# Reordering the start of an attention kernel: K transposes ahead of x, half of V behind a swap, and w2 in pieces

## The chip, the cores and the metric

The kernel runs on one core of one Trainium2 chip. The metric is the time of one execution on the device in microseconds (us). The profile's span, from the first to the last instruction, is 1.8 us shorter than that time. PE is TensorE, PEld its weight loads, DVE VectorE, ACT ScalarE, POOL GpSimd; SPq is the queue of SyncE, which issues most DMAs.

## The reference

```
xn  = layernorm(A_x)                                   # 2048 x 640
q   = xn @ wq                                          # 32 heads of 192
p   = softmax(q @ k_cache.T / sqrt(192))               # 2048 keys per head
s   = (p @ v_cache, heads side by side) @ wo
g   = silu((silu(xn @ w1) * (xn @ w3)) @ w2)
out = A_x + s * g
```

All inputs are bfloat16. The part with w1, w3 and w2 uses the same normalised x as the attention.

## The kernel before

The kernel walks 32 heads x 4 query blocks of 512 rows x 8 pairs of key tiles. For each pair TensorE computes scores, ScalarE the exponential, and TensorE the product with V. At the start of each query block TensorE also computes the projection of the next head ("line 424"), from the normalised and transposed x (`xnT`) and from a copy with its two 64-row halves swapped (`xnS`).

Head 0 has to be started from nothing. Its order is written by hand (shortened here; cuts are marked with dots):

```python
def head_start():
    load_x(0, 0, 2); load_x(0, 2, 4)      # x block 0, SyncE's queue
    load_k0(0)                            # kn: first half of head 0's K
    load_w0()                             # GpSimd's queue
    load_k0(1)
    load_x(1)
    load_v(0)                             # both halves of head 0's V
    turn_over(40)                         # 40 matmuls that only warm TensorE up ("fillers")
    ...                                   # layer norm of x block 0 on DVE, ACT, POOL
    pk0 = ...
    ln_turn(0, 0, nc.scalar.copy)         # transpose x rows 0-255 on TensorE; ScalarE copies (line 354)
    turn_over(4)
    turn_k0(pk0, 0, (0, 1))               # transpose K (line 271)
    turn_over(4)
    ln_turn(0, 1, nc.vector.tensor_copy)  # x rows 256-511
    turn_k0(pk0, 0, (2, 3))
    turn_over(4)
    turn_k0(pk1, 1, (0, 1))
    swap_halves(0)                        # xnS <- xnT, two DMAs on SyncE's queue
    copy_k0(nc.scalar.copy, pk0, 0, 0); copy_k0(nc.scalar.copy, pk0, 0, 1)
    copy_k0(nc.vector.tensor_copy, pk1, 1, 0)
    for g in range(2, NQB):
        load_x(g)                         # x blocks 2 and 3
    project_first()                       # head 0, query block 0 (line 391)
    ...
    ln_norm(1, 0, nc.vector); ln_norm(1, 1, nc.vector)
    ln_turn_dma(1, 0); ln_turn_dma(1, 1)  # x block 1, first half: transposed by DMA into xnT
    ln_stats(1, 3)
```

Later, in query block 0 of head 0: `ln_stats(2, 0)` (VectorE, needs x block 2) stands in program order ahead of the cast of head 1's first projection (line 429); that cast frees a buffer in PSUM, the memory that TensorE writes its results to, that the next x transposes (line 354) want.

## Time and profile before

Three runs took 1942.91, 1943.74 and 1945.92 us. The kernel is limited by TensorE almost everywhere. First the share of TensorE and weight loads on the page of the kernel before, then busy time by stretch (columns: stretch, its length, then busy us and instruction count for PE, PEld, DVE, ACT, POOL; granted clock, DMA share, GB/s):

```profile
PE 1930.7 (99%) x27289; PEld 1318.9 (68%) x27289; DVE 654.6 (34%) x997; ACT 1181.4 (61%) x1278; POOL 282.0 (15%) x501
...
0.00:24.00 24.00, 19.02 (x223) 14.43 (x225) 15.76 (x49) 12.92 (x17) 8.64 (x16) 1.00 1.01 235
64.00:1624.00 1560.00, 1560.00 (x24100) 1064.46 (x24096) 533.77 (x742) 1104.27 (x1170) 254.88 (x455) 1.00 0.36 82
```

From 64 us to 1624 us TensorE has no gap at all, so no change to loads there can shorten anything. In the first 24 us it is idle for 5 us, while the DMA engines are saturated (share 1.01). The waits of PE in the first 30 us (who waits, for what: us, times, longest):

```profile
PE pk L568 <- POOL ident_bf masks.py:199: 2.8, 1, 2.8
PE ps L424 <- DMA xnS<-xnT: 1.1, 1, 1.1
PE pst L354 <- DVE xn L346: 0.7, 1, 0.7
```

The first line is the start-up before any filler can run. The second is the wait that the change aims at. Lines picked from the timeline around it (start, length, engine, line, operation; in brackets the idle time ahead of it and what ended it); here and below, lines in between are left out:

```profile
7.91 0.81 PE L354 MATMUL pst<-ident_bf,xn 128*128 128x128 bf16 x10 [0.69 <-DVE xn L346]
8.78 0.61 PE L271 MATMUL pk<-ident_bf,kn 128*128 128x128 bf16 x8
11.12 0.66 SPq L364 DMA_DIRECT2D xnS<-xnT  x1
11.82 0.62 SPq L365 DMA_DIRECT2D xnS<-xnT  x1
20.14 0.38 PE L424 MATMUL ps<-xnT,W 64*128 64x512 bf16 x1
21.58 0.39 PE L424 MATMUL ps<-xnS,W 64*128 64x512 bf16 x2 [1.07 <-DMA xnS<-xnT]
22.89 0.89 DVE L316 BATCH_NORM_STATS2 stats<-x_all 128x6 f32<-128x320 bf16 x2 [0.70 <-DMA x_all<-in_A_x_dram]
```

The swap is issued at 11.12 and 11.82 us and lands at 21.54 (9.7 us after its issue), behind V, whose second half lands at 18.10. TensorE arrives at head 1's projection at 20.14 and continues at 21.58.

### The profile page before, as it was taken

The page shows a single profiled execution, that of the slowest core. Times are in us where ns is not written, and L with a number is a line of the kernel's source. Part 1 is how long each engine was busy: PE and PEld are TensorE (multiplying, and loading weights), DVE is VectorE, ACT ScalarE, POOL GpSimd, SP SyncE. Part 2 cuts the span into 40 slices and gives each one's busy share as a digit, 9 for nine tenths or more (in the row PEclk, how much of TensorE's full clock was granted, in tenths as well). Part 3 has the DMA queues.
Part 4 walks back from the last instruction along what each step waited for, and adds up shares of the span by engine and source line. Part 5 has one row for each costly group of instructions (what it writes and reads, how often), then busy time and mean ns, then how long its engine had stood idle before and what let it go on. Part 6 is the DMA issues. An engine that isn't in the chain of part 4 may idle for free.

```text
span 1940.9 us, 59694 instructions
## 1 busy us (share of the span) xinstructions
PE 1930.7 (99%) x27289; PEld 1318.9 (68%) x27289; DVE 654.6 (34%) x997; ACT 1181.4 (61%) x1278; POOL 282.0 (15%) x501
## 2 busy tenths in 40 slices
PE   8999999999999999999999999999999999999998
PEld 6666666666666666666666666666666666577776
DVE  7333333333333333333333333333333334521111
ACT  5667776767776767776777777677767677210000
POOL 3111111111111111111111111111111110000000
PEclk9999999999999999999999999999999999999999
DMA  8743433323233424353434343434333220937883
GB/s 177 132 100 65 99 70 74 89 55 92 59 91 68 94 64 101 68 162 68 101 64 101 68 101 68 99 66 100 69 69 94 55 73 2 256 70 137 153 152 60
DMA packets 394563, 178.98 MB, mean 92 GB/s; under 512 B 341536, under 2 KB 382752, under 8 KB 394304
## 3 DMA queue, kind: packets, MB, share of 16 engines
q1 hardware_dynamic: 372384, 126.76, 30.6%
q0 software_dynamic: 19472, 45.71, 9.9%
q8 instruction: 215, 3.52, 0.8%
q10 hardware_dynamic: 2448, 2.62, 0.4%
q14 instruction: 44, 0.36, 0.1%
HBM read 52.82 MB, written 27.79 MB: 42 GB/s over the span
## 4 chain that ended last, share of the span: by engine, by line
PE 98%; DMA 1%; DVE 0%; ACT 0%; issue 0%; SPq 0%; DVEq 0%; ACTq 0%
PE obank L516 35%; PE st L487 33%; PE ps L424 14%; PE ps_s L111 11%; PE ps_f L728 3%; PE ps_gu L702 1%; PE st L488 1%; DMA xnS<-xnT 1%; PE ps L410 0%; DVE stats L316 0%; DMA x_all<-in_A_x_dram 0%; PE pst L354 0%; ACT pT L490 0%; ACT KW L277 0%; DVE osum L526 0%; PE pk L271 0%
## 5 line engine op out<-in xcount | busy, mean ns | idle before, releaser
L490 ACT ACTIVATE pT<-st 128x1024 bf16<-128x1024 f32 x1024 | 1047.2, 1023 | 250.8 <-PE st L488 234.8
L516 PEld LDWEIGHTS <-pT 64*128 64x128 bf16 x16384 | 713.8, 94 | 242.1 <-ACT pT L490 0.2
L516 PE MATMUL obank<-vt,pT 64*128 64x193 bf16 x16384 | 852.0, 243 | 0.0
L487 PE MATMUL st<-qC,KW 64*128 64x512 bf16 x2046 | 605.6, 376 | 0.0
L525 DVE COPY osum<-obank 128x772 f32<-128x772 f32 x128 | 123.1, 962 | 788.8 <-PE obank L516 788.8
L488 PE MATMUL st<-qB,KW 64*128 64x512 bf16 x1024 | 385.0, 376 | 0.0
L487 PE MATMUL st<-qA,KW 64*128 64x512 bf16 x1022 | 384.3, 376 | 0.4 <-ACT pT L490 0.3
L488 PE MATMUL st<-qC,KW 64*128 64x512 bf16 x1022 | 384.3, 376 | 0.0
L488 PE MATMUL st<-qA,KW 64*128 64x512 bf16 x1022 | 384.3, 376 | 0.0
L487 PEld LDWEIGHTS <-KW 64*128 64x128 bf16 x3068 | 278.0, 94 | 153.5 <-issue 2.1
L424 PE MATMUL ps<-xnT,W 64*128 64x512 bf16 x1280 | 297.2, 376 | 0.0
L424 PE MATMUL ps<-xnS,W 64*128 64x512 bf16 x1280 | 296.0, 376 | 1.1 <-DMA xnS<-xnT 1.1
L488 PEld LDWEIGHTS <-KW 64*128 64x128 bf16 x3068 | 278.0, 94 | 1.0 <-issue 0.6
L377 POOL DMA_DIRECT2D qC<-qA x124 | 65.4, 527 | 1286.9 <-DVE rl_all L532 1270.5
L430 ACT CAST qB<-ps 128x512 bf16<-128x512 f32 x131 | 76.8, 586 | 229.7 <-PE ps L424 224.2
L111 PE MATMUL ps_s<-wo_sb,oT 128*128 128x256 bf16 (+3 forms) x1536 | 208.8, 299 | 0.0
L424 PEld LDWEIGHTS <-W 64*128 64x128 bf16 x2560 | 122.9, 94 | 122.6 <-issue 1.4
L111 PEld LDWEIGHTS <-oT 128*128 128x128 bf16 x1536 | 148.4, 98 | 60.4
L526 DVE TENSOR_TENSOR osum<-osum,obank 128x772 f32<-128x772 f32 x128 | 122.7, 959 | 13.4
L533 DVE TENSOR_TENSOR ostage<-osum,rl_all 128x768 bf16<-128x768 f32 x128 | 122.7, 958 | 4.4
L465 DVE SCALAR_TENSOR_TENSOR hT<-pt,qB 64x512 bf16<-64x512 bf16 x64 | 43.8, 684 | 199.4 <-ACT pt L464 199.4
L429 DVE CAST qA<-ps 128x512 bf16<-128x512 f32 x131 | 90.6, 692 | 25.0 <-PE ps L410 7.2
(84 smaller groups left out, 623.6 us busy)
## 6 DMA issues: line engine op xcount, KB each, us to landing
vt<-in_A_v_cache_dram SPq DMA_DIRECT2D x64, 384.0 KB, 5.5
o_scr<-ostage SPq DMA_DIRECT2D x16, 1536.0 KB, 10.3
qC<-qA POOLq DMA_DIRECT2D x248, 64.0 KB, 2.0
qC<-qB POOLq DMA_DIRECT2D x124, 64.0 KB, 2.2
wo_sb<-in_A_wo_dram POOLq DMA_DIRECT2D x1, 7680.0 KB, 34.6
W<-in_A_wq_dram POOLq DMA_DIRECT2D x32, 160.0 KB, 3.4
W<-in_B_w_dram POOLq DMA_DIRECT2D x32, 80.0 KB, 3.2
W<-in_A_wq_dram POOLq DMA_DIRECT2D x32, 80.0 KB, 2.9
```

Of the source, the lines that this page charges most:

```text
L111: nc.tensor.matmul(ps[:, 0:w], lhsT=oT[:, k, :], rhs=wo_sb[:, k, c0:c1], start=(k == 0), stop=(k == OC - 1))
L377: nc.gpsimd.dma_start(out=qC[0:64, half, :], in_=qAB[half][64:P, :])
L424: nc.tensor.matmul(ps[:, r * 512:(r + 1) * 512], lhsT=W[rows, j, :], rhs=xs[rows, j // 2, qs], start=(j == 0), stop=(j == 2 * DC - 1))
L429: a = nc.vector.tensor_copy(out=qAB[0][:], in_=ps[:, 0:512])
L430: b = nc.scalar.copy(out=qAB[1][:], in_=ps[:, 512:1024])
L487: nc.tensor.matmul(st2[:, 0:512], lhsT=ka, rhs=qa, start=r == 0 and nr == 3, stop=r == nr - 1)
L488: nc.tensor.matmul(st2[:, 512:1024], lhsT=kb, rhs=qb2, start=r == 0 and nr == 3, stop=r == nr - 1)
L490: nc.scalar.activation(out=pT2[:], in_=st2[:], func=ACT.Exp, scale=att_scale)
L516: nc.tensor.matmul(obanks[r][:, j * 256:j * 256 + DH + 1], lhsT=pT2[r * 64:(r + 1) * 64, t * 512 + j * P:t * 512 + (j + 1) * P], rhs=vt[r ...
L525: nc.vector.tensor_copy(out=osum[:], in_=ov[0])
L526: nc.vector.tensor_tensor(out=osum[:], in0=osum[:], in1=ov[1], op=ALU.add)
L533: nc.vector.tensor_tensor(out=ostage[:, qb * 4:qb * 4 + 4, hg * DH:(hg + 1) * DH], in0=osum[:, :, 0:DH], in1=rl.unsqueeze(2).to_broadcast( ...
```

## The change

Three things: the K transposes of head 0's first half go ahead of the x transposes, with six fillers fewer, to use TensorE's idle gap; the second half of V is issued behind the swap; w2 (needed only at 1675 us) is loaded as six DMAs, not one.

```diff
-    def load_v(h):
+    def load_v(h, halves=(0, 1)):
...
-        for t in range(2):
+        for t in halves:
...
-            nc.sync.dma_start(out=wrest["w2"], in_=B_w2.rearrange("(c p) d -> p c d", p=P))
+            for c0, c1 in _pieces(FC, -(-FC // 6)):
+                nc.sync.dma_start(out=wrest["w2"][:, c0:c1, :], in_=...[:, c0:c1, :])
...
-        load_v(0)
-        turn_over(40)
+        load_v(0, (0,))
+        turn_over(34)
...
+        turn_k0(pk0, 0, range(4))
+        copy_k0(nc.scalar.copy, pk0, 0, 0)
+        turn_over(4)
         ln_turn(0, 0, nc.scalar.copy)
-        turn_over(4)
-        turn_k0(pk0, 0, (0, 1))
-        turn_over(4)
+        turn_k0(pk1, 1, (0, 1))
         ln_turn(0, 1, nc.vector.tensor_copy)
-        turn_k0(pk0, 0, (2, 3))
-        turn_over(4)
-        turn_k0(pk1, 1, (0, 1))
         swap_halves(0)
-        copy_k0(nc.scalar.copy, pk0, 0, 0)
         copy_k0(nc.scalar.copy, pk0, 0, 1)
         copy_k0(nc.vector.tensor_copy, pk1, 1, 0)
+        load_v(0, (1,))
```

More of the change, by code (lines that the diff above doesn't have):

```diff
@@ L544, in loads_after @@
             wrest["w2"] = w_all[:, 0:FC * D].rearrange("p (c d) -> p c d", d=D)
-            nc.sync.dma_start(out=wrest["w2"], in_=B_w2.rearrange("(c p) d -> p c d", p=P))
+            for c0, c1 in _pieces(FC, -(-FC // 6)):
+                nc.sync.dma_start(out=wrest["w2"][:, c0:c1, :], in_=B_w2.rearrange("(c p) d -> p c d", p=P)[:, c0:c1, :])
             o1 = FC * D
```

## The prediction

> **What bounds the kernel now.** TensorE. The profile's first part has PE busy 1930.7 of 1940.9 us (99%), and the chain of waits is 98% PE. By stretches, PE is busy 19.0 of the first 24 us and 1599.9 of the next 1600 us. Projection blocks (line 424) start 12.69 us apart throughout, also around 848 us, where w2 is loaded. So only the first 24 us hold anything to win: about 5 us, 2.8 of them a wait for the identity matrix, which the change does not touch.
>
> **Where the start is lost.** In the timeline, the normalised x of block 0 is ready at 11.03 us; the swap of halves (xnS) is issued at 11.12 and 11.82 and lands at 21.54. It sits behind V: the second V half, issued at 3.83, lands at 18.10. PE reaches head 1's projection at 20.14 and waits for xnS (wait list: "PE ps L424 <- DMA xnS<-xnT: 1.1"); it restarts at 21.58.
>
> **What the change does.**
> - V: 384 KB leave the queue ahead of the swap. The Trainium skill, "DMA: Bandwidth & Descriptors", section on queues, rings and completion order, says each DMA engine consumes a ring in order; the landings above agree. I estimate the swap to land at 16 to 19 us, before PE needs it. The wait of 1.1 us goes.
> - But the same bytes still precede x block 2: it lands near 22.9 us, as before. VectorE's first statistics of that block (22.89 us, "<- DMA x_all") stand ahead of its cast of head 1's first projection, which frees the PSUM buffer of the next transposes (line 354, 25.14 us). So the cast can hardly end before 24.6 us (22.87 + 0.44 twice + 0.21 + 0.69), and PE, early, waits there: some 0.4 us of the 1.1 remain.
> - K turns: six warm-up matmuls fewer (0.107 us each), then 16 K transposes ahead of the x transposes. kn's first half lands at 7.85 us, just when the x transposes now start (7.91). So 16 x 0.056 us plus four fillers push those to about 9.0 us; ScalarE copies K first (1.01 us), then x at about 10.1 (1.23 us). First projection about 11.3 us instead of 11.12; swap issued 0.3 to 0.6 us later. A small loss, hidden by what follows.
> - Warm-up: PE reached full clock at 7.3 us, shortly after the 40 fillers ended (pitch 107 ns, then 56 ns). With 34 they end near 6.4. The skill's "TensorE: Matmul & The Clock Gate", section on the clock gate, has a free-running activity window of about 3.4 us; some runs may stay slow for one more window, which could cost 1 to 2 us.
> - w2 in six pieces: five more issues on SyncE at 848 us; nothing waits for w2 until 1675 us. Zero.
>
> **Sum.** -0.4 us: **1943.3 us**, range 1940.9 to 1946.0 (the three runs of before alone spread over 3.0 us). Faster by over 2%: 0.005; within 2%: 0.99; slower by over 2%: 0.005.
>
> **What would show it right or wrong.** PE's wait on xnS gone, xnS landed before 19 us; x block 2 still landing at 22.5 to 23.5 us; a new PE wait before line 354 near 24 us on VectorE's cast; the first x transposes at 8.8 to 9.2 us; block spacing still 12.69 us.
>
> **What would make it wrong.** x block 2 landing a microsecond earlier (then up to 1.3 us are gained); V's second half landing after about 25 us (a new wait in the value products); the clock staying halved at 8 us (slower by 1 to 2 us); the K half landing late, delaying the x transposes, since it now stands ahead of them.

## More of the kernel before

`project0(1)` (line 410) projects head 0's query block 1 and needs all of x block 1 transposed.

## The result, and the profile after

| | runs | median us | lowest | highest |
|---|---|---|---|---|
| before | 6 | 1943.53 | 1942.91 | 1945.92 |
| after | 6 | 1942.64 | 1941.67 | 1944.41 |

The ratio is 0.9994 (interval 0.9981 to 1.0007). Ratios here are the mean time of one kernel's fast runs over that of the other's in the same rounds, so not quite the ratio of the medians.

The median is 0.9 us lower, but the profiled execution of after is the slowest of its six (1944.41 us, span 1942.6) and slower than before's profiled one. Its stretches, then PE's waits in the first 30 us:

```profile
0.00:24.00 24.00, 18.06 (x199) 14.43 (x202) 14.04 (x44) 12.95 (x16) 8.62 (x16) 1.00 0.84 227
64.00:1624.00 1560.00, 1560.00 (x24102) 1065.15 (x24100) 533.49 (x742) 1103.59 (x1171) 255.35 (x455) 1.00 0.36 82
```

```profile
PE pk L569 <- POOL ident_bf masks.py:199: 2.8, 1, 2.8
PE pk L271 <- DMA kn<-in_A_k_cache_dram: 2.4, 1, 2.4
PE ps L410 <- DMA xnT<-xn: 0.7, 1, 0.7
```

The wait on xnS is gone. Two others stand in its place: 2.4 us on kn and 0.7 us on the transposed x block 1. The timeline of the same execution:

```profile
2.77 3.81 PE L569 MATMUL pk<-ident_bf 128*128 128x128 bf16 x34 [2.77 <-POOL ident_bf masks.py:199]
8.94 1.89 PE L271 MATMUL pk<-ident_bf,kn 128*128 128x128 bf16 x16 [2.35 <-DMA kn<-in_A_k_cache_dram]
10.62 0.63 PE L569 MATMUL pk<-ident_bf 128*128 128x128 bf16 x4
11.04 1.19 PE L354 MATMUL pst<-ident_bf,xn 128*128 128x128 bf16 x10
14.19 0.64 SPq L364 DMA_DIRECT2D xnS<-xnT  x1
22.42 0.38 PE L424 MATMUL ps<-xnT,W 64*128 64x512 bf16 x1
29.02 2.32 PE L410 MATMUL ps<-xnT,W 128*128 128x512 bf16 x9 [0.66 <-DMA xnT<-xn]
```

The x transposes start at 11.04 us, not at 7.91: kn landed at 8.89 us (7.85 before), and TensorE was still at half clock: 16 K transposes took 1.89 us, 107 ns apart, where 8 took 0.61 us before (56 ns apart; the last one's end adds some 0.2 us to either). The trace's record of the full clock begins at 12.01 us (7.30 before). The 3.1 us add up, as an estimate: 1.0 for the later start, 20 x 0.056 = 1.1 for the K transposes and fillers now ahead at full clock, and 20 x 0.051 = 1.0 more for the half clock.

Is this execution typical? A second profile of the same kernel (after_again, below) says no. There kn landed at 5.76 us, the clock was full at 5.65, and PE's waits in the first 30 us are these:

```profile
PE pst L354 <- DVE qA L429: 0.8, 1, 0.8
PE pk L271 <- DMA kn<-in_A_k_cache_dram: 0.7, 1, 0.7
PE ps L391 <- DMA W<-in_A_wq_dram: 0.7, 1, 0.7
PE ps L410 <- DVE ve L319: 0.7, 1, 0.7
```

The wait on VectorE's cast (L429) before the x transposes (L354) is the one that was predicted. The chain of waits of that execution names its source, x block 2 (start, length, what):

```profile
13.97 8.75 DMA x_all<-in_A_x_dram
```

and the timeline shows the cast held behind that block's statistics, then TensorE held by the cast, and then the wait that was not predicted, line 410:

```profile
22.74 0.89 DVE L316 BATCH_NORM_STATS2 stats<-x_all 128x6 f32<-128x320 bf16 x2 [0.53 <-DMA x_all<-in_A_x_dram]
23.79 0.64 DVE L429 CAST qA<-ps 128x512 bf16<-128x512 f32 x1
24.48 0.73 PE L354 MATMUL pst<-ident_bf,xn 128*128 128x128 bf16 x10 [0.75 <-DVE qA L429]
27.32 2.32 PE L410 MATMUL ps<-xnT,W 128*128 128x512 bf16 x10 [0.68 <-DVE ve L319]
```

(The last release is put down to VectorE here. Line 410 also needs the second DMA transpose of x block 1, which landed at 27.18; the other profile of after names that DMA.)

### A yardstick that is finer than the clock on the wall

The timed runs of one kernel spread over 2 to 4 us, so half a microsecond is hard to time. But in all fourteen profiles the span from the start of the fourth projection block (the fourth group of line 424, near 64 us) to the end lies between 1876.9 and 1877.2 us. All but 0.3 us of what differs between kernels or executions happens before it. That start divides further: TensorE's arrival at head 1's first projection, plus 42.48 us (the shortest seen from there to the fourth block, with no wait but the usual ones), plus a remainder. The remainder is mostly waits, but not all: in before it is 1.26 us, and the one listed wait there is 1.07.

| profile of | fillers | kn landed | full clock at | arrival | remainder | fourth block | span |
|---|---|---|---|---|---|---|---|
| before | 40 | 7.85 | 7.30 | 20.14 | 1.26 | 63.88 | 1940.90 |
| after | 34 | 8.89 | 12.01 | 22.42 | 0.75 | 65.65 | 1942.65 |
| after_again | 34 | 5.76 | 5.65 | 20.08 | 1.42 | 63.98 | 1940.92 |
| v_only | 40 | 8.27 | 8.78 | 20.60 | 0.38 | 63.46 | 1940.40 |
| k_only | 34 | 6.90 | 6.76 | 19.98 | 0.92 | 63.38 | 1940.34 |
| w2_only | 40 | 6.93 | 8.20 | 20.06 | 1.02 | 63.56 | 1940.51 |
| after_fill60 | 60 | 6.04 | 5.78 | 19.71 | 1.09 | 63.28 | 1940.30 |
| after_fill0 | 0 | 5.73 | 11.70 | 20.36 | 0.94 | 63.78 | 1940.82 |
| v_behind_x2 | 40 | 7.86 | 7.54 | 20.25 | 1.27 | 64.00 | 1941.01 |
| x3_late | 40 | 5.89 | 7.42 | 20.46 | 0.00 | 62.94 | 1940.03 |
| x3_late_k60 | 60 | 7.57 | 6.44 | 20.39 | 0.03 | 62.90 | 1939.94 |
| after_x3 | 34 | 7.65 | 11.17 | 21.26 | 0.07 | 63.81 | 1940.74 |
| after_kn_late | 34 | 10.22 | 14.17 | 23.84 | 0.93 | 67.25 | 1944.43 |
| before_kn_late | 40 | 10.88 | 8.73 | 22.71 | 0.00 | 65.19 | 1942.33 |

"Full clock" is the beginning of the trace's record of full clock; where it could be checked, the distance of the matmuls changes from 107 to 56 ns there. One profile is one execution, and kn's landing alone differs by 3 us between executions of kernels whose queue up to kn is the same. So a row is read by its waits, not by its last column alone.

### The profile page after: what moved, and what is told of

Its sections match the earlier page's. It is cut to its first block, busy times and chain, and to the rows that moved or that the text cites. A ratio compares the mean times of both kernels' runs of the same rounds, so it can differ in the third digit from the quotient of the medians.

```text
span 1942.6 us, 59661 instructions
## 1 busy us (share of the span) xinstructions
PE 1930.4 (99%) x27267; PEld 1319.7 (68%) x27275; DVE 654.3 (34%) x997; ACT 1180.5 (61%) x1278; POOL 282.5 (15%) x501
## 4 chain that ended last, share of the span: by engine, by line
PE 98%; DMA 1%; DVE 1%; ACT 0%; issue 0%; SPq 0%; DVEq 0%; ACTq 0%
PE obank L516 35%; PE st L487 33%; PE ps L424 14%; PE ps_s L111 11%; PE ps_f L727 3%; PE ps_gu L701 1%; PE st L488 1%; DMA kn<-in_A_k_cache_dram 0%; PE ps L410 0%; DMA xnT<-xn 0%; DVE stats L316 0%; PE ps L391 0%; PE pk L271 0%; ACT xnT L356 0%; DVE xn L346 0%
## 5 line engine op out<-in xcount | busy, mean ns | idle before, releaser
L111 PE MATMUL ps_s<-wo_sb,oT 128*128 128x384 bf16 (+3 forms) x1535 | 208.8, 299 | 0.1
L429 DVE CAST qA<-ps 128x512 bf16<-128x512 f32 x131 | 90.6, 692 | 25.6 <-PE ps L410 7.8
```

Of the source, the lines that this page charges most:

```text
L111: nc.tensor.matmul(ps[:, 0:w], lhsT=oT[:, k, :], rhs=wo_sb[:, k, c0:c1], start=(k == 0), stop=(k == OC - 1))
L429: a = nc.vector.tensor_copy(out=qAB[0][:], in_=ps[:, 0:512])
```

## The experiments

Theory A is the prediction's: the swap lands earlier, and x block 2 takes part of that back. Theory B: the gain comes from the K order. Theory C: the clock and kn's landing decide more than the change does. Each kernel was timed in five runs; before was timed in nine on the same chip. All results were correct.

| kernel | median us | lowest to highest | before, same chip | ratio, 95% interval |
|---|---|---|---|---|
| v_only | 1942.85 | 1942.03 to 1944.50 | 1943.28 | 0.9998, 0.9985 to 1.0012 |
| k_only | 1942.59 | 1942.11 to 1943.14 | 1943.28 | 0.9996, 0.9983 to 1.0010 |
| after_fill60 | 1942.13 | 1941.63 to 1945.22 | 1943.28 | 0.9997, 0.9984 to 1.0011 |
| v_behind_x2 | 1942.58 | 1941.70 to 1942.79 | 1943.28 | 0.9994, 0.9980 to 1.0008 |
| x3_late | 1942.25 | 1941.51 to 1943.28 | 1943.18 | 0.9994, 0.9980 to 1.0008 |
| x3_late_k60 | 1941.97 | 1941.66 to 1943.00 | 1943.18 | 0.9994, 0.9980 to 1.0007 |
| after_fill0 | 1943.80 | 1942.07 to 1944.69 | 1943.18 | 1.0001, 0.9987 to 1.0014 |
| after_again | 1942.70 | 1942.10 to 1943.51 | 1943.18 | 0.9996, 0.9982 to 1.0009 |
| w2_only | 1942.56 | 1942.24 to 1943.51 | 1943.09 | 0.9999, 0.9985 to 1.0012 |
| after_kn_late | 1945.33 | 1944.25 to 1946.29 | 1943.09 | 1.0010, 0.9997 to 1.0024 |
| before_kn_late | 1944.09 | 1942.62 to 1945.00 | 1943.09 | 1.0004, 0.9990 to 1.0017 |
| after_x3 | 1942.51 | 1942.08 to 1943.15 | 1943.09 | 0.9997, 0.9984 to 1.0011 |

No interval excludes 1.

### v_only: the second half of V behind the swap, nothing else

```diff
-        load_v(0)
+        load_v(0, (0,))
...
         copy_k0(nc.vector.tensor_copy, pk1, 1, 0)
+        load_v(0, (1,))
```

> Only the second V half moves behind the swap; K order, 40 fillers and w2 as before. Theory A (the change gains through the swap): TensorE's wait on xnS before head 1's projection is gone, xnS lands before 19 us, x block 2 still near 22.9 us; the fourth projection block (63.88 us in the profile of before) starts 0.4 us earlier if the clock is full at 8 us; time -0.4 us, -0.2 to -1.0. Theory B (the gain comes from the K order): the time is that of before within 0.2 us. Theory C (the state of TensorE's clock and kn's landing at 8 us decide more than the change): the profile shows which state this execution had; executions of one kernel spread over 2 to 3 us.

Measured: the swap lands at 17.94 and 19.32 us (19.92 and 21.54 before), x block 2 at 22.20, and the wait on xnS is gone. The fourth block is at 63.46, 0.42 earlier, which is the expected number but not by the expected way: the condition for it, a full clock at 8 us, did not hold (8.78), the arrival was 0.46 us later than before's, and the predicted wait at line 354 did not occur. A wait of 0.32 us before line 410 appears instead, which no theory had.

### k_only: the K order and the 34 fillers, nothing else

The change with its V and w2 parts undone.

> Only the K order and the 34 fillers of the change; V and w2 as before. Theory A: the wait of 1.1 us on xnS is still there, the x transposes start at 9 us or later, the time is that of before or up to 0.5 us longer. Theory B: 0.9 us shorter than before. Theory C: TensorE idles from 6.5 us until kn lands (8 to 9 us), and where the clock is not yet full by then the transposes run at 107 ns and head 1's projection starts about 2 us later: 1 to 2 us longer than before in those executions, so a wider spread.

Measured: the wait on xnS is still there (0.71 us). In this execution kn landed at 6.90, soon after the last filler, the clock was full, and the x transposes started at 8.08 us, not at 9 or later. Arrival is 0.16 us earlier than before's. The fairer partner is w2_only (below), which has before's order and in which kn landed at nearly the same moment (6.93): against it the arrival is 0.08 us earlier. The five runs show no slow execution, so the wide spread expected of theory C did not come.

### after_fill60: the changed kernel with 60 fillers

```diff
-        turn_over(34)
+        turn_over(60)
```

> The changed kernel with 60 warm-up matmuls in place of 34, so that TensorE is busy until kn lands. Theory C: the clock is full before 9.5 us in the profile, the 16 K transposes run at 56 ns, head 1's projection starts at 20 to 20.8 us instead of 22.42 in the profile of after; time 0.5 to 1 us under the changed kernel's, thus about 1.4 to 2 us under before's, with a narrower spread. If the clock's phase does not matter (theory A alone): the same time as the changed kernel, 0.9 us under before.

Measured: the clock was full at 5.78 us and the arrival, 19.71 us, is the earliest of all. Yet the fourth block is only 0.6 us ahead of before's, because 1.1 us of waits follow (line 354, 0.56, and line 410, 0.58). The spread was not narrower: one run took 1945.22 us. So the fillers do not remove the slow executions.

### v_behind_x2: V's second half behind the swap and behind x block 2

```diff
-        load_v(0)
+        load_v(0, (0,))
...
-        for g in range(2, NQB):
-            load_x(g)
+        load_x(2)
+        load_v(0, (1,))
+        load_x(3)
```

> The kernel before with the second V half behind the swap and also behind x block 2 (V is needed only at about 25 us). Theory A with its second step (x block 2 caps the gain through VectorE's statistics): x block 2 lands at 20 to 21.5 us, VectorE's cast of head 1's first projection is not held by it, TensorE waits for neither; the fourth projection block starts 1.1 to 1.3 us earlier than in v_only's rival state (62.6 to 62.8 us with a full clock at 8 us), time 1.1 to 1.3 us under before. If x block 2 does not cap: the same as v_only.

Measured: x block 2 lands at 21.56 us (20 to 21.5 expected) and the wait at line 354 is gone, as expected. But the fourth block is at 64.00 us, no earlier than before. PE's wait list shows where the gain went, and the timeline when:

```profile
PE ps L410 <- DMA xnT<-xn: 1.3, 1, 1.3
```

```profile
23.96 0.73 PE L354 MATMUL pst<-ident_bf,xn 128*128 128x128 bf16 x10
27.38 2.32 PE L410 MATMUL ps<-xnT,W 128*128 128x512 bf16 x10 [1.26 <-DMA xnT<-xn]
```

TensorE reaches the transposes 1.2 us earlier than before (25.15) and line 410 0.1 us later (27.24). The DMA transposes of x block 1, issued at 19.1 and 20.6 us, land at 26.62 and 27.24, after x block 3 (24.47). This led to theory A2: whatever the order of swap, V and x ahead of these transposes, the bytes ahead are the same; only what moves behind them helps.

### x3_late: as v_behind_x2, and x block 3 behind the DMA transposes

```diff
-        load_x(3)                     # as in v_behind_x2
...
         ln_turn_dma(1, 1)
+        load_x(3)
```

> Before's order and 40 fillers; V's second half behind x block 2, and x block 3 issued only behind the two DMA transposes of block 1. Theory A2 (in v_only and v_behind_x2 TensorE's wait moved from xnS to the transposed block 1, line 410, because everything queued ahead of the two DMA transposes is the same number of bytes whatever its order; only what is moved behind them counts): the transposes land at 23 to 24.5 us instead of 26.6 and 27.2, no wait before line 410, the fourth projection block starts at 62.3 to 62.8 us (63.88 before, 63.46 v_only, 64.00 v_behind_x2); time 1.0 to 1.5 us under before. Rival (the wait at line 410 has another cause, or another wait follows): the fourth block stays at 63.3 to 64 us.

Measured: the fourth block starts at 62.94 us, and the wait is gone:

```profile
24.16 0.73 PE L354 MATMUL pst<-ident_bf,xn 128*128 128x128 bf16 x10
26.25 2.33 PE L410 MATMUL ps<-xnT,W 128*128 128x512 bf16 x10
```

Between v_behind_x2 and this kernel only the place of x block 3 differs, so A2 is supported in its main point, by one profile of each. Its numbers were a little off: the transposes land at 25.11 and 25.68 us, 1.5 us earlier rather than the 3 expected, which suffices because line 410 is reached at 26.25; and the fourth block misses the expected range by 0.14, with a later arrival (20.46).

The other half of A2, that the same bytes ahead mean the same landing, does not hold. In three of the fourteen profiles (before, k_only, after_fill0) the second of these transposes lands 1.2 to 1.3 us after the last load ahead of it; in the other eleven it takes 2.6 to 4.1 us. w2_only, with before's order of loads, is among the eleven: 26.80 us against before's 25.80. What the extra 1.3 us or more is, no run here settles. v_behind_x2 and x3_late both have it (2.77 and 2.71 us), so they can be compared; before and v_behind_x2 cannot. after_fill0 is without it, and there the transposes land at 24.69 us and line 410 does not wait for them, although x block 3 is ahead.

### x3_late_k60: the changed kernel with 60 fillers, and x block 3 behind the transposes

```diff
-        turn_over(34)
+        turn_over(60)
...
-        load_v(0, (1,))
-        for g in range(2, NQB):
-            load_x(g)
+        load_x(2)
+        load_v(0, (1,))
...
         ln_turn_dma(1, 1)
+        load_x(3)
```

> The changed kernel with 60 fillers and x block 3 behind the two DMA transposes, V's second half behind x block 2. Theory A2: no wait on xnS, on line 410 or on line 354; fourth block at 61.8 to 62.4 us if kn has landed by 8 us; time 1.5 to 2 us under before, the fastest of all. Rival: no better than after_fill60 (63.28 us).

Measured: 0.03 us of waits after arrival, the fourth block at 62.90 us, the lowest span and the lowest median (1941.97 us; 1.2 us under before, 0.7 under after_again on the same chip). It is no better than x3_late by the profile, though: with kn at 7.57 us the x transposes started at 8.98, and the arrival is only 0.07 us earlier than x3_late's, where kn landed at 5.89.

### after_fill0: the changed kernel without the 34 fillers

```diff
-        turn_over(34)
```

> The changed kernel without its 34 first fillers. Theory C (clock): TensorE starts its K transposes at half clock when kn lands and gets full clock only 3 to 6 us later, in every execution; x transposes at 107 ns; fourth block at 65 to 66 us as in the profile of after (65.65); time 1.5 to 2.5 us over the changed kernel's faster executions, about 1944.2. If the clock does not matter (late kn alone made the profile of after slow): the time of the changed kernel, 1942.6.

Measured: the clock stayed half until 11.70 us, as expected, but the arrival was at 20.36 us and the fourth block at 63.78, far from the 65 to 66 expected. kn landed at 5.73 here; the 16 K transposes were done, at half speed, before x was ready at 7.89. Against after_again, with kn at nearly the same moment and a full clock, the arrival differs by 0.28 us. (Most of the 0.94 us that follow is a wait of 0.86 us at 41.2 us for the DMA transposes of x block 2, seen in no other profile.) So the half clock cost little in this execution, in which TensorE waited for data anyway; theory C in the form "the clock alone, in every execution" falls. But the profile fell on one of the two fast runs of this kernel (1942.59 us). The other three took 1943.80, 1943.85 and 1944.69 us and were not profiled, and the median, 1943.80, is 1.1 us over after_again's.

### after_again: the changed kernel, unaltered

> The changed kernel unaltered, for a second profile and more times. Theory C: executions fall in two groups, near 1942.3 (clock full by 8 us) and near 1944.3 (not full until 11 to 12 us), about half each[...]; this profile shows one of the two, with the fourth block near 63.3 or near 65.6 us. If theory C is wrong: the profile has a late clock and yet the fourth block near 63.3 us, or a full clock and the block near 65.6.

Measured: the profile shown above. No run near 1944.3 among these five; of all eleven runs of the changed kernel two are (1944.41 and 1944.25). The two groups of about half each that theory C expected are not what the runs show. The profile also contradicts the narrower form of theory C: full clock at 5.65 us, yet the fourth block at 63.98, not 63.3, because waits at lines 354 and 410 add 1.4 us.

### w2_only: w2 in six pieces, nothing else

> Before with w2 in six pieces alone. All theories: no change; from the fourth projection block to the end the span is 1877.0 us as in every profile so far, projection blocks 12.69 us apart around 848 us; the time is before's within its own spread (median within 0.5 us). It also gives a second profile of before's head: theory D (the executions differ in the first 64 us alone) expects its time minus 1878.8 to be the start of the fourth block.

Measured: nothing, in the trace. The load of w2 is issued from 843.9 us on (the 848 us of the prediction is the load of w1 and w3 behind it). TensorE in the stretch that follows, before, then w2_only:

```profile
845.00:900.00 55.00, 55.00 (x862) 37.82 (x858) 17.96 (x25) 39.78 (x44) 8.39 (x15) 1.00 0.57 148
```

```profile
845.00:900.00 55.00, 55.00 (x856) 37.63 (x854) 17.71 (x25) 39.74 (x43) 8.42 (x15) 1.00 0.57 147
```

There is no idle time in either. The fourth block starts at 63.56 us, and the time less 1878.8 is 63.57, as theory D (the executions differ in the first 64 us alone) expects. Its median was 0.53 us under before's all the same, while the ratio of the means is 0.9999. That is a measure of what five runs can say: a difference of half a microsecond in the medians means nothing here. (The expected limit of 0.5 us was missed by 0.03.)

### after_kn_late and before_kn_late: kn issued behind x block 1

Theory E: the changed order is more exposed to a late kn than the order before. Both kernels get the same edit:

```diff
-        load_k0(0)
         load_w0()
-        load_k0(1)
         load_x(1)
+        load_k0(0)
+        load_k0(1)
```

> The changed kernel with kn's two loads issued behind x block 1, so that kn always lands late (10 to 12 us). Theory E (the profile of after was slow because the K transposes now stand ahead of the x transposes, so a late kn delays the whole head; and the idle gap leaves the clock half): the x transposes start 1 to 2.2 us after kn's landing, the first projection 4 to 5 us after it, fourth block at 66 to 68.5 us, time 2 to 4 us over the changed kernel.

> Before with the same late kn. Theory E: the first x transposes still start at 7.8 to 7.9 us at full or nearly full clock and ScalarE copies them at once; only the second group waits; the first projection comes about 2 to 3 us after kn's landing, that is 1 to 2 us less lost than in after_kn_late. Rival (both orders are equally exposed to kn): both lose the same.

Measured, the timeline of after_kn_late and then of before_kn_late:

```profile
10.27 1.89 PE L271 MATMUL pk<-ident_bf,kn 128*128 128x128 bf16 x16 [3.69 <-DMA kn<-in_A_k_cache_dram]
11.95 0.63 PE L569 MATMUL pk<-ident_bf 128*128 128x128 bf16 x4
12.38 1.27 PE L354 MATMUL pst<-ident_bf,xn 128*128 128x128 bf16 x10
14.97 0.27 PE L391 MATMUL ps<-xnT,W 128*128 128x256 bf16 x1
```

```profile
7.81 1.15 PE L354 MATMUL pst<-ident_bf,xn 128*128 128x128 bf16 x10 [0.58 <-DVE xn L346]
10.93 0.62 PE L271 MATMUL pk<-ident_bf,kn 128*128 128x128 bf16 x8 [1.75 <-DMA kn<-in_A_k_cache_dram]
13.76 1.47 PE L391 MATMUL ps<-xnT,W 128*128 128x256 bf16 x12
```

In the changed order everything waits for kn: the x transposes start 2.2 us and the first projection 4.75 us after its landing (10.22). In the order before, the first x transposes run at 7.81, and the first projection comes 2.9 us after kn's landing (10.88). The gap between the last filler and kn (3.7 us) also leaves the clock half until 14.17; before's order, which works at 7.81, has it full at 8.73 (so its first x transposes were still partly slow, against what was expected). The arrival is 13.6 us after kn in one and 11.8 in the other: the changed order loses 1.8 us more to the same late load. The medians differ by 1.2 us, as expected.

### after_x3: the changed kernel with x block 3 behind the DMA transposes

```diff
         for g in range(2, NQB):
-            load_x(g)
+            load_x(2)                 # block 2 alone
...
         ln_turn_dma(1, 1)
+        load_x(3)
```

> The changed kernel unaltered except that x block 3 is issued behind the two DMA transposes of block 1. Theory A2: TensorE's wait before line 410 (0.66 and 0.68 us in the two profiles of after) is gone; the wait on VectorE's cast before line 354 may stay (0.75 us); time 0.3 to 0.7 us under the changed kernel, about 1942.2. Rival: the wait at line 410 stays.

Measured: the wait at line 410 is gone, and only 0.13 us is left at line 354. The profile fell on an execution with a late clock (11.17 us; the gap between the fillers and kn was 1.1 us), so the arrival was late (21.26), and still the fourth block is at 63.81 us, because nothing waits afterwards.

This profile also gives the cost of the half clock with an ordinary kn. x3_late_k60 has the same K order, 60 fillers, kn at 7.57 us (7.65 here) and a full clock at 6.44. The K and first x transposes of after_x3, then of x3_late_k60:

```profile
7.69 1.89 PE L271 MATMUL pk<-ident_bf,kn 128*128 128x128 bf16 x16 [1.11 <-DMA kn<-in_A_k_cache_dram]
9.80 1.27 PE L354 MATMUL pst<-ident_bf,xn 128*128 128x128 bf16 x10
```

```profile
7.86 1.06 PE L271 MATMUL pk<-ident_bf,kn 128*128 128x128 bf16 x16
8.98 0.72 PE L354 MATMUL pst<-ident_bf,xn 128*128 128x128 bf16 x10
```

The x transposes start 0.82 us later at half clock, and the arrival is 0.87 us later. (The place of V's second half differs too, but neither arrival waits for it.)

In time, the median is 1942.51, against 1942.68 for the eleven runs of the changed kernel, taken elsewhere: inconclusive in time, clear in the waits.

## Why the prediction was right or wrong

The time lies in the range and within 0.7 us of the number. For the number this is luck in part: the range is 5 us wide for an effect of 0.4, and the two profiles of after have the fourth block 0.1 and 1.8 us later than before's, not 0.4 earlier. What was right is that the change is lost in the spread of the executions, and which waits go and come. Point by point:

- **Only the start matters, w2 is worth nothing.** Right: 1876.9 to 1877.2 us from the fourth block on in every profile; w2_only leaves TensorE without a gap.
- **The swap lands at 16 to 19 us and the wait of 1.1 us goes.** The wait is gone in every profile with V moved. The landing was a little later than estimated: second half at 19.55 and 19.89 us in the two profiles of after.
- **x block 2 takes part of it back, through VectorE's cast and the buffer of line 354.** Right where the head was punctual: in after_again the block lands at 22.72 and TensorE waits 0.75 us at 24.48. In the other profile of after the wait is absent (0.12 us), because TensorE was itself 2.3 us late.
- **-0.4 us in sum.** Not shown. v_only gives -0.42 us at the fourth block, but from other terms (see there). The sum lacked one: the DMA transposes of x block 1, which land behind x block 3 on the same queue. The wait before line 410 was 0.66 and 0.68 us in the two profiles of after, and 1.26 in v_behind_x2; it is absent in x3_late, x3_late_k60 and after_x3. The estimate stopped at the first new wait. The size of this one varies with the unexplained 1.3 us in the landing of the transposes. Taken together, the listed waits after arrival are 0.71 to 1.07 us in the three profiles with V in its old place and kn in its ordinary one (before, k_only, w2_only), and 0.32 to 1.43 in the five with V right behind the swap and all other loads of the start in their old order (after, after_again, v_only, after_fill60, after_fill0). One profile each, and different arrivals: moving V shows no clear gain.
- **The K order costs 0.1 to 0.2 us, hidden.** This step was mis-sized, because it took kn's landing from one execution (7.85 us). kn lands between 5.73 and 8.89 us in kernels that issue it alike. With an early kn the order gains a little (after_again: arrival 0.06 us earlier than before's; k_only: 0.08 earlier than w2_only's); with kn at 8.89 and the half clock 2.3 us of arrival were lost. The last of the prediction's warnings named this, and after_kn_late shows it.
- **The clock may stay half for a window more.** It did, in two of the four profiles with 34 fillers and an ordinary kn load (12.01 and 11.17 us, against 5.65 and 6.76), and in none of the six with 40 and before's order of transposes (at most 8.78). Its cost depends on kn: 0.28 us of arrival with kn at 5.73 (after_fill0 against after_again), 0.87 with kn at 7.65 (after_x3 against x3_late_k60), each from one pair of profiles, and about 1.0 by the estimate for the profile of after. So "1 to 2 us" was at the upper end.
- **"x block 2 landing a microsecond earlier, then up to 1.3 us are gained".** Not as a remedy by itself: in its one profile, v_behind_x2 brings it in at 21.56 us and gains nothing, for the term left out above.

Where does the 0.9 us between the medians come from? This stays open. The two profiles of after have the fourth block at 63.98 and 65.65 us, neither earlier than before's 63.88, and w2_only, which does nothing, also has a median 0.5 us lower. Over all runs on all chips, before has 33 with a mean of 1943.45 and after 11 with 1942.82. Four of the 33 runs of before exceed 1945 us, none of after's; no profile fell on such an execution of before, so what makes them slow is not known. One run of after_fill60 exceeds it too (1945.22).

A version that is ahead of both in the profile exists: x3_late keeps before's K order, which does not wait for kn first, puts V behind x block 2, and x block 3 behind the DMA transposes (1942.25 us median; fourth block 62.94). x3_late_k60 adds the changed K order and is level with it. By the timer both are the same as before within 2%.

## What to carry to other kernels

When loads share one saturated queue, reordering them may only choose who waits, as it did here: list every consumer of the queue in order of need, and move the transfers that nobody needs yet behind the last one that somebody does. Put work that depends on a load with an uncertain landing behind work whose data is already there, not ahead of it. Where one execution differs from the next by more than the change is worth, find a point in the trace after which all executions agree, and compare kernels by what happens before it.

## What the Trainium skill lacked or had wrong

- "TensorE: Matmul & The Clock Gate", section on the clock gate: it gives a free-running window of about 3.4 us, but not how busy the window has to be. Taking 3.41 us windows back from the moment of full clock in the fourteen profiles, and counting 107 ns for each matmul at half clock, TensorE was busy for 0.76 to 1.00 of each window that led to full clock, and for at most 0.76 of each earlier one (with the profile's own modelled ends: 0.82 to 1.00, and at most 0.78). This is an estimate built on the page's window. In the traces, 34 fillers (3.8 us) followed by an idle gap of 1.1 to 3.7 us had full clock only at 11.2 to 14.2 us, and 40 followed by 0.6 to 0.7 us had it by 8.8. Its distances of 107 and 56 ns agree with the trace.
- The same page advises keeping TensorE busy to pass the window. It does not say how much less the half clock may cost while data is what TensorE waits for: 0.28 us of arrival in the profile of after_fill0, 0.87 in that of after_x3.
- "DMA: Bandwidth & Descriptors", section on queues, rings and completion order: each engine consumes a ring in order, which the landings agree with (x block 3 at 24.47 us, the transposes issued behind it at 26.62 and 27.24, v_behind_x2). No page says how much the landing of one load varies between executions: kn, issued at 1.68 us, landed between 5.73 and 8.89 us in the twelve profiles that issue it there.
- The page on the clock does not name this reading of the trace: the granted clock of a stretch is shown as 1.00 in the first microseconds, where the fillers are 107 ns apart; the clock's record only begins when full clock is granted (12.01 us in the profile of after).
